# A fused attention and MLP kernel: the first batch's norms reordered, and two thirds of the second batch's norms moved into its own attention

## The chip, the cores and the metric

The kernel runs on one core of one Trainium2 chip. The metric is device time in microseconds, the median of several executions. One execution was also taken by the hardware profiler; all durations below come from that one. Batches are numbered from 1 here (the code's `b` from 0).

## The reference

Attention with normed queries and keys, then an MLP. Shapes: 8 batches, 12 heads, 448 positions, head size 64, so 3584 tokens of width 768, and 2048 inner features. All inputs and the output are float32.

```python
def rmsnorm(x, g):
    rms = np.sqrt(np.mean(x * x, axis=-1, keepdims=True) + 1e-06)
    return x / rms * g
q_n, k_n = (rmsnorm(q, g_q), rmsnorm(k, g_k))
scores = np.matmul(q_n, k_n.transpose(0, 1, 3, 2)) / np.sqrt(64)
attn = softmax(scores)
x = np.matmul(attn, v)           # heads side by side: (3584, 768)
h = x @ w_in
out = gelu_tanh(h) @ w_out
```

## The kernel before, in words

**Tiling.** A batch's 448 positions are 4 tiles of 112. Heads go in pairs (6 pairs), since two heads of 64 fill 128 partitions. Loads, squares and norms go in chunks of 4 heads (2 pairs), 3 chunks to a batch. `rawqk` holds 4 chunks of q and 4 of k in float32, used in turn.

**Norm.** For a piece of q or k: squares (`square`, L113, on ACT or POOL), their sums over the head (`total`, L122, DVE), the root as exp(-0.5 ln(.)) (`rsqrt`, L129, two ACT instructions, `lg` and `rinv`), and the product with the root, which also casts to bfloat16 (`normed`, L144, DVE or POOL). Gains g_q and g_k are folded into one column `gcol` that multiplies the transposed keys only.

**Transposes.** Scores need q and k with the head on partitions. Batch 1 transposes on PE (`trans`, L153): 8 matmuls into one PSUM tile, then a copy to `qT` and the gain product to `kT`. Later batches use DMA transposes issued by SP (`dma_trans`, L178), one for q and one for k of a chunk, and `gain` (L189) on DVE. kT is one buffer for all batches, and so is qT.

**Attention.** `scores` (L196) makes a 112 x 896 tile of scores for a pair and a key tile, two matmuls, and one exp on ACT (L206). There are 24 such tiles in a batch. Two PSUM tiles (`ps_s`) take turns, so a score matmul waits for the exp two before it. The exp subtracts a constant `shift` made of the largest gain product in place of the row's maximum. `pair_sums` (L219) then makes the sums over keys (`what` 0, matmul with ones; on DVE two 32x32 transposes and a reciprocal, L241 to L243) and the product with V (`what` 1, then L236). A slot is half of a pair: two score tiles, and in batch 1 one of the two `pair_sums`. There are 12 slots.

**MLP.** `mm1` makes 128 inner features of a batch (6 matmuls and a gelu into `g`); in batch 1 `mm1_pair` (L290) makes 256 at a time. `mm2` (L261) makes 128 tokens by 384 outputs from 16 matmuls. Two batches share the halves of `g`; the mm2 of the batch before is spread over the attention of the next by counts (`attention`, L314).

**Order.** The order is written by hand: each engine executes its own instructions as the program emits them, and waits on semaphores. `plan` (L382) hangs small steps on slot numbers. `first_attention` (L353) runs batch 1's attention with the lists `side` (ahead of the slot's scores), `mid` (between its two score tiles) and `late` (behind `pair_sums`); then follows mm1 of batch 1 with the list `m1` by inner step, then batch 2's attention with its own `side`. SP issues all loads of q and k, the DMA transposes and the outputs, in one queue. POOL issues V, w_in and w_out (cast to bfloat16 on the way), between its squares and norms. A SP or POOL instruction whose buffer isn't free holds all that stands behind it.

**What the steps touch, before.** The start, L440 to L476: the gain column, `gall` by five DVE transposes, `shift`, then the first pair's squares, sums, root, norm, transposes. Batch 1's other pairs: squares and norms on POOL, roots in `mid`, transposes in `late`, pair hp + 1 in slot 2 hp. w_in comes in four parts (L472, L487, L490, L491), w_out in two halves (L494, L497). Batch 2: squares on POOL in slots 8 to 11 (four of six in unused parts of `g`), one root for all three chunks in mm1 (L508, with an activation table load before and after, since gelu and exp don't share a table), 12 norms on DVE (L513), the six DMA transposes, and only then (L541) batch 3's loads.

Of the kernel before, what the change touches and what calls it, by code (L numbers as in the profile page):

```python
# [16 lines left out]
def kernel(  # L17
# [54 lines left out]
    gall = consts.tile([128, 2, 32], F32)  # L72
    shift = consts.tile([P, 1], F32)
    eps = consts.tile([P, 1], F32)
    win = wts.tile([128, HP, d_ff], BF16)
# [63 lines left out]
    def idle(n, w):  # L139

        for _ in range(n):
            nc.tensor.matmul(w, zeros[:, :128], zeros, start=True, stop=True)
# [207 lines left out]
            pair_sums(b, HP - 1, what)  # L350
        upto(quota)

    def first_attention(side, mid, late):  # L353


        warm = {}
        for i in range(HP * 2):
            for fn in side.get(i, ()):
                fn()
            scores(0, i // 2, 2 * (i % 2))  # L360
            for fn in mid.get(i, ()):
                fn()
            scores(0, i // 2, 2 * (i % 2) + 1)
            if i < 2:
                warm[i] = ps_o.tile([128, S], F32, tag=f"o{i}", name=f"o{i}")
                idle((6, 2)[i], warm[i])
            if i >= 2:
                pair_sums(0, i // 2 - 1, i % 2, waits=1)
            for fn in late.get(i, ()):
                fn()  # L370
            if i == 1:
                idle(4, warm[i])
        nc.scalar.preload_act_table_set(GELU_SET)
        square(1, 2, "k", nc.scalar)
        pair_sums(0, HP - 1, 0)
        mm1_pair(0, range(HP - 1))
        pair_sums(0, HP - 1, 1)
        mm1_pair(1, range(HP - 1))
        for i in range(2):
            mm1_pair(i, range(HP - 1, HP))  # L380

    def plan(*entries):  # L382
        steps = {}
# [12 lines left out]
        qh[i]()  # L396
        kh[i]()
    loads(0, 2)
    loads(1, 0)
    loads(1, 1)  # L400
    load_v(0, 0, CH)
    nc.vector.memset(eps, 1e-6)
    nc.vector.memset(ones, 1.0)

    def pair(hp):
        return hp // (CH // 2), hp % (CH // 2), slice(2 * (hp % (CH // 2)), 2 * (hp % (CH // 2)) + 2)
# [30 lines left out]
            moe_w_out[:, i * HD:(i + 1) * HD].rearrange("(f p) d -> p f d", p=128),  # L437
        )

    w = ps_m.tile([128, 512], F32, tag="mm", name="w")[:, :S]  # L440
# [5 lines left out]
    for r in range(4):  # L446
        at = (r ^ 1) * 32
        nc.vector.transpose(
            gall[r * 32:(r + 1) * 32, 1], gcol[at:at + 32].to_broadcast([32, 32])
        )  # L450

    nc.vector.tensor_reduce(
        shift, gall[:P].rearrange("p a d -> p (a d)"), axis=AX.X, op=ALU.max,
        apply_absolute_value=True,
    )
    nc.vector.tensor_scalar(shift, shift, -(D ** 0.5), 60.0, op0=ALU.mult, op1=ALU.add)
    nc.vector.tensor_scalar(shift, shift, 0.0, None, op0=ALU.min)
    squares0(0, nc.scalar)
    totals0(0)
    square(0, 0, "q", nc.scalar, slice(2, 4))  # L460
    rsqrt0(0)
    square(0, 0, "k", nc.scalar, slice(2, 4))
    total(0, 0, "q", slice(2, 4))
    normed0(0, nc.vector)
    total(0, 0, "k", slice(2, 4))
    trans(0, 0, ps_m)
    idle(4, ps_m.tile([128, 512], F32, tag="mm", name="w")[:, :S])
    rsqrt0(1)
    squares0(2, nc.gpsimd)
    square(0, 1, "q", nc.gpsimd, slice(2, 4))  # L470
    w_in_part(0, 4)
    normed0(1, nc.gpsimd)  # L472
    square(0, 1, "k", nc.gpsimd, slice(2, 4))
    load_v(0, CH, CH)
    squares0(4, nc.gpsimd)
    totals0(2)  # L476


    free = g[:P].rearrange("p f s -> p (f s)")
    for i, (n, c) in enumerate((n, c) for c in (1, 2) for n in "qk"):  # L480
        at = nf * 2 * S - (4 - i) * 2048
        sqs[n, 1, c] = free[:, at:at + 2048].bitcast(F32).rearrange(
            "p (h t d) -> p h t d", h=CH, t=NK
        )

    side = [(1, lambda: totals0(3)),
            (2, lambda: normed0(2, nc.gpsimd), lambda: w_in_part(1, 4),  # L487
             lambda: squares0(5, nc.gpsimd), lambda: totals0(4)),
            (4, lambda: normed0(3, nc.gpsimd), lambda: load_v(0, 2 * CH, CH),
             lambda: w_in_part(2, 4), lambda: totals0(5)),  # L490
            (6, lambda: normed0(4, nc.gpsimd), lambda: w_in_part(3, 4)),  # L491
            (7, lambda: loads(1, 2)),
            (8, lambda: normed0(5, nc.gpsimd), lambda: square(1, 0, "q", nc.gpsimd)),
            (9, lambda: square(1, 0, "k", nc.gpsimd), lambda: w_out_part(0)),  # L494
            (10, lambda: square(1, 1, "q", nc.gpsimd), lambda: total(1, 0, "q")),
            (11, lambda: square(1, 1, "k", nc.gpsimd), lambda: total(1, 0, "k"),
             lambda: load_v(1, 0, CH), lambda: w_out_part(1),  # L497
             lambda: square(1, 2, "q", nc.gpsimd))]
    mid = [(1, lambda: rsqrt0(2))] + [
        (2 * hp - 3, lambda hp=hp: rsqrt0(hp)) for hp in range(3, HP)]  # L500
    late = [(1, lambda: trans(0, 1, ps_m))] + [
        (2 * hp, lambda hp=hp: trans(0, hp + 1, ps_m)) for hp in range(1, HP - 1)]
    first_attention(plan(*side), plan(*mid), plan(*late))
    for c in (1, 2):
        for n in "qk":
            total(1, c, n)

    def rsqrt1():  # L508
        nc.scalar.preload_act_table_set(EXP_SET)
        rsqrt(1)  # L510
        nc.scalar.preload_act_table_set(GELU_SET)

    def normed1(c):  # L513
        for j in range(CH // 2):
            for n in "qk":
# [100 lines left out]
```

## Time and profile before

| | us |
|---|---|
| median of 3 runs | 459.52 (458.99 to 459.62) |
| the profiled execution, its time | 458.26 |
| its span (first to last instruction) | 456.5 |
| first exp starts | 13.99 |
| last exp of batch 1 ends | 44.09 |
| mm1 of batch 1 done on PE | 65.5 |
| first scores of batch 2 | 67.17 |
| batch 2's attention done, mm1 of batch 2 starts | 103.3 |
| PE busy | 435.2 (95% of the span) |
| ACT busy | 306.2 (67%) |
| DVE busy | 252.7 (55%) |
| POOL busy | 154.2 (34%) |
| granted PE clock, mean | 0.996 |

The busy times are means over stages that differ. The first 103 us hold all loads of weights, the first batch without any other work to fill PE, and the second batch's norms; the remaining 353 us repeat one pattern. The profile's 40 slices are 11.4 us each.

### The profile page before, as it was taken

Reading aid. Unit: us, or ns where it says so; the run is one execution under the profiler, and the core shown is the slowest. Engines: PE = TensorE matmul, PEld = TensorE weight load, DVE = VectorE, ACT = ScalarE, POOL = GpSimd, SP = SyncE. Lnnn points to the kernel's source line nnn. Section 1 sums busy time; section 2 is a strip of 40 time slices with the busy share of each in tenths; the row PEclk is TensorE's granted clock in tenths of the full one; section 3 lists DMA queues with packets and bytes.
Section 4 is the critical chain, followed back from the end, with each engine's and each line's share of the span. In section 5 each row is a group of like instructions: output and inputs, shape, how many; then the busy total and the mean of one; then the engine's idle time right before and its main releaser. Section 6 shows DMA issues by size and latency. Waiting matters only on the chain.

```text
span 456.5 us, 7031 instructions
## 1 busy us (share of the span) xinstructions
PE 435.2 (95%) x2766; PEld 212.7 (47%) x2766; DVE 252.7 (55%) x429; ACT 306.2 (67%) x406; POOL 154.2 (34%) x136
## 2 busy tenths in 40 slices
PE   5789979899999999999999999999999999999995
PEld 2233434345544554445544554455544554455563
DVE  5667663963397536874297536874288602862000
ACT  3679567665888577875888577875788447873410
POOL 4989405554400923046400923046400920000000
PEclk9899999999999999999999999999999999999999
DMA  8999999918951586317951586316751541111022
GB/s 225 231 233 166 203 200 233 209 34 150 251 93 36 136 183 131 80 36 180 219 93 36 127 191 117 95 36 166 154 93 36 107 51 34 36 37 34 1 69 69
DMA packets 84193, 54.92 MB, mean 120 GB/s; under 512 B 41152, under 2 KB 80576, under 8 KB 84160
## 3 DMA queue, kind: packets, MB, share of 16 engines
q1 hardware_dynamic: 65792, 42.68, 39.2%
q0 software_dynamic: 18208, 11.80, 18.4%
q8 instruction: 21, 0.34, 0.3%
q14 instruction: 12, 0.10, 0.1%
q10 hardware_dynamic: 160, 0.00, 0.0%
HBM read 45.61 MB, written 11.01 MB: 124 GB/s over the span
## 4 chain that ended last, share of the span: by engine, by line
PE 84%; DVE 4%; ACT 4%; DMA 3%; POOL 3%; issue 1%; SPq 1%; DVEq 0%; POOLq 0%; ACTq 0%
PE o L268 32%; PE h L250 28%; PE o L229 13%; PE sc L202 9%; ACT ex L206 3%; DMA rawq<-in_q_dram 2%; POOL sq L120 2%; PE hh L298 1%; DVE ss L125 1%; DVE nrmq L147 1%; DVE nrmk L147 1%; DMA kT<-nrmk 1%; POOL nrmq L147 0%; POOL nrmk L147 0%; PE tp L164 0%
## 5 line engine op out<-in xcount | busy, mean ns | idle before, releaser
L206 ACT ACTIVATE ex<-sc,shift 112x896 bf16<-112x896 f32 x192 | 182.9, 1003 | 32.6 <-PE sc L202 31.5
L268 PE MATMUL o<-wout,g 128*128 128x384 bf16 x896 | 160.7, 327 | 0.0
L250 PE MATMUL h<-xT,win 128*128 128x448 bf16 x672 | 128.3, 352 | 0.0
L268 PEld LDWEIGHTS <-g 128*128 128x128 bf16 x896 | 80.6, 98 | 71.0 <-issue 24.1
L254 ACT ACTIVATE g<-h 128x448 bf16<-128x448 f32 x112 | 60.9, 544 | 76.3 <-PE h L250 73.4
L250 PEld LDWEIGHTS <-win 128*128 128x128 bf16 x672 | 65.8, 98 | 61.0
L147 POOL TENSOR_TENSOR nrmq<-rawq,rinv 112x512 bf16<-112x512 f32 x41 | 44.0, 1091 | 133.1 <-issue 123.2
L125 DVE TENSOR_REDUCE ss<-sq 112x16 f32<-112x1024 f32 (+1 forms) x50 | 53.5, 1086 | 64.1 <-ACT sq L118 55.1
L278 DVE COPY osb<-o 128x384 f32<-128x384 f32 x52 | 28.7, 551 | 75.4 <-PE o L268 75.4
L202 PE MATMUL sc<-qT,kT 64*128 64x448 bf16 x384 | 56.4, 357 | 5.8 <-ACT ex L206 2.0
L217 DVE TENSOR_TENSOR es<-ex 112x896 bf16<-112x896 bf16 x72 | 47.1, 654 | 2.7 <-ACT ex L206 1.7
L241 DVE STREAM_TRANSPOSE st<-o 128x448 f32<-128x448 f32 x48 | 31.1, 649 | 30.1 <-PE o L229 30.1
L120 POOL TENSOR_TENSOR sq<-rawq 112x1024 f32<-112x1024 f32 (+1 forms) x13 | 21.7, 1671 | 74.6 <-DMA rawq<-in_q_dram 43.0
L229 PE MATMUL o<-ex,vb 112*64 112x448 bf16 x384 | 44.8, 353 | 1.4 <-DVE xT L236 1.4
L147 POOL TENSOR_TENSOR nrmk<-rawk,rinv 112x512 bf16<-112x512 f32 x41 | 44.0, 1090 | 0.0
L202 PEld LDWEIGHTS <-kT 64*128 64x128 bf16 x384 | 16.6, 93 | 45.0 <-issue 36.0
L236 DVE TENSOR_TENSOR xT<-o,rb 128x448 bf16<-128x448 f32 x48 | 30.0, 624 | 6.2 <-PE o L229 1.8
L243 DVE STREAM_TRANSPOSE rb<-rc 128x448 f32<-128x448 f32 x48 | 31.0, 645 | 1.6
L229 PEld LDWEIGHTS <-vb 112*64 112x64 bf16 x384 | 22.5, 109 | 14.4 <-issue 3.5
L120 POOL TENSOR_TENSOR sq<-rawk 112x1024 f32<-112x1024 f32 (+1 forms) x13 | 21.7, 1668 | 5.2 <-DVE ss L125 4.3
L229 PE MATMUL o<-es,ones 112*64 112x448 bf16 x144 | 21.6, 366 | 0.1
L229 PEld LDWEIGHTS <-ones 112*64 112x64 bf16 x240 | 11.8, 108 | 18.7 <-issue 16.2
(52 smaller groups left out, 205.1 us busy)
## 6 DMA issues: line engine op xcount, KB each, us to landing
rawq<-in_q_dram SPq DMA_DIRECT2D x22, 448.0 KB, 5.4
rawk<-in_k_dram SPq DMA_DIRECT2D x22, 448.0 KB, 5.8
vb<-in_v_dram POOLq DMA_DIRECT2D x6, 672.0 KB, 7.2
win<-in_moe_w_in_dram POOLq DMA_DIRECT2D x4, 768.0 KB, 9.4
wout<-in_moe_w_out_dram POOLq DMA_DIRECT2D x2, 1536.0 KB, 13.5
out_dram<-osb SPq DMA_DIRECT2D x8, 336.0 KB, 2.8
out_dram<-osb SPq DMA_DIRECT2D x8, 288.0 KB, 2.7
out_dram<-osb SPq DMA_DIRECT2D x8, 240.0 KB, 2.7
```

What stands on the lines that cost most here:

```text
L120: eng.tensor_mul(sq, raw, raw)
L125: nc.vector.reduce_sum(sss[b][:, c, "qk".index(n), hs], sqs[n, b, c][:, hs], axis=AX.X)
L147: eng.tensor_mul(nrms[n, b, c][:, j].rearrange("p t a d -> p a t d"), raws[n, b, c][:, 2 * j:2 * j + 2], rinvs[b][:, c, "qk".index(n), 2 * ...
L202: nc.tensor.matmul(sc[:, a, :S], kT[r, hp, kt], qT[b][r, hp], start=True, stop=True,)
L206: nc.scalar.activation(exs[b, hp][:, kt], sc[:P, :, :S], AF.Exp, scale=scale, bias=shift)
L217: nc.vector.tensor_add(ess[b, hp][:, i], ex[:, 2 * i], ex[:, 2 * i + 1])
L229: nc.tensor.matmul(o[a * D:(a + 1) * D], vb[b % 2][:, 2 * hp + a, i] if what else ones, e[:, i, a], start=(i == 0), stop=(i == n - 1),)
L241: nc.vector.transpose(st.rearrange("p a b -> p (a b)"), o)
L243: nc.vector.transpose(oas["rb"], rc.to_broadcast([128, S // 32, 32]))
L250: nc.tensor.matmul(h[:, :S], win[:, c, f * 128:(f + 1) * 128], xT[b][:, c], start=(c == 0), stop=(c == HP - 1),)
L254: nc.scalar.activation(g[:, f, (b % 2) * S:(b % 2 + 1) * S], h[:, :S], AF.Gelu_apprx_tanh)
L268: nc.tensor.matmul(o[:, :HD], g[:, f, i * 128:(i + 1) * 128], wout[:, f, half * HD:(half + 1) * HD], start=(f == 0), stop=(f == nf - 1),)
```

## The change

At the start, squares, sums and root of the first pair come ahead of the gain column; `shift` comes from one small matmul (ones by a diagonal of gains in bfloat16, hence a margin of 2^-8) in place of five DVE transposes. The other squares of batch 1's chunks 2 and 3 mostly go to unused parts of `g` and not to the two-buffer pool. The second pair's norm goes from POOL to DVE. Batch 1's transposes move from slot 2 hp - 2 to slot 2 hp - 1, ahead of the product with V (pair 3: behind it). The warming matmul in front of `pair_sums` stays only in slots 2 to 5. w_in's second part moves behind the fifth pair's norm, its third and fourth behind the last norm and two squares of batch 2. The pairs of mm1 are no longer cut around the last product with V.

Batch 2's chunk 1 gets a root of its own in slot 11 and is normed on DVE and transposed at the start of mm1. Chunks 2 and 3 get their root (no table loads of its own) and their norms, now on POOL, at the start of batch 2's attention, the transposes of chunk 2 behind that and those of chunk 3 in slot 4. The loads of batch 3's chunks 1 and 2 stand on SP right behind the first transposes, its chunk 3 behind the second, and batch 4's chunk 1 (slot 1) and the first output pieces also stand ahead of the third. The sums of batch 3's squares come some slots later. A dummy `rawqk` tile is taken, so that the chunks keep the buffers that they had.

```diff
-    def first_attention(side, mid, late):
+    def first_attention(side, mid, early, late):
...
-            if i >= 2:
-                pair_sums(0, i // 2 - 1, i % 2, waits=1)
-            for fn in late.get(i, ()):
+            for fn in early.get(i, ()):
                 fn()
             if i == 1:
                 idle(4, warm[i])
+            if i >= 2:
+                pair_sums(0, i // 2 - 1, i % 2, waits=i < 6)
+            for fn in late.get(i, ()):
+                fn()
         nc.scalar.preload_act_table_set(GELU_SET)
         square(1, 2, "k", nc.scalar)
-        pair_sums(0, HP - 1, 0)
-        mm1_pair(0, range(HP - 1))
-        pair_sums(0, HP - 1, 1)
-        mm1_pair(1, range(HP - 1))
+        for what in range(2):
+            pair_sums(0, HP - 1, what)
         for i in range(2):
-            mm1_pair(i, range(HP - 1, HP))
+            mm1_pair(i)
...
-    loads(1, 0)
-    loads(1, 1)
-    load_v(0, 0, CH)
+    for n in "qk":
+        rawqk.tile([P, CH, NK, D], F32, tag=f"raw{n}", name=f"raw{n}")
...
-    idle(20, w)
+    idle(16, ps_m.tile([128, 512], F32, tag="mm", name="w")[:, :S])
+    squares0(0, nc.scalar)
+    totals0(0)
+    rsqrt0(0)
     for a in range(2):
         nc.vector.tensor_mul(gcol[a * D:(a + 1) * D], grow[:, 0:1], grow[:, 1:2])
-    nc.vector.transpose(gall[:, 0], gcol.to_broadcast([128, 32]))
...
+    nc.vector.tensor_scalar(gdiag, ident[:D, :D], gcol[:D, 0:1], None, op0=ALU.mult)
+    gall = ps_o.tile([128, S], F32, tag="o1", name="gall")
+    nc.tensor.matmul(gall[:P, :D], rows, gdiag, start=True, stop=True)
...
+    side = [(1, lambda: normed0(1, nc.vector), lambda: total(0, 1, "k", slice(0, 2)),
+             lambda: loads(1, 0)),
+            (2, lambda: rsqrt0(2), lambda: normed0(2, nc.gpsimd),
+             lambda: load_v(0, CH, CH), lambda: square(0, 2, "k", nc.gpsimd, slice(0, 2)),
+             lambda: totals0(3)),
+            (4, lambda: normed0(3, nc.gpsimd), lambda: squares0(5, nc.gpsimd),
+             lambda: totals0(4), lambda: loads(1, 1)),
+            (6, lambda: normed0(4, nc.gpsimd), lambda: w_in_part(1, 4),
+             lambda: load_v(0, 2 * CH, CH), lambda: totals0(5)),
+            (8, lambda: normed0(5, nc.gpsimd), lambda: square(1, 0, "q", nc.gpsimd),
+             lambda: square(1, 0, "k", nc.gpsimd), lambda: w_in_part(2, 4),
+             lambda: w_in_part(3, 4), lambda: loads(1, 2)),
+            (10, lambda: square(1, 1, "q", nc.gpsimd), lambda: total(1, 0, "k")),
+            (11, lambda: square(1, 1, "k", nc.gpsimd), lambda: w_out_part(0),
+             lambda: load_v(1, 0, CH), lambda: square(1, 2, "q", nc.gpsimd),
+             lambda: w_out_part(1))]
+    mid = [(0, lambda: rsqrt0(1))] + [(2 * hp - 3, lambda hp=hp: rsqrt0(hp)) for hp in range(3, HP)]
+    early = [(2 * hp + 1, lambda hp=hp: trans(0, hp + 1, ps_m)) for hp in (0, 2, 3, 4)]
+    mid.append((11, lambda: rsqrt(1, 0)))
+    late = [(3, lambda: trans(0, 2, ps_m)), (9, lambda: total(1, 0, "q"))]
...
         if b == 0:
-            m1 = [(2, rsqrt1)]
-            for c in range(NCH):
-                m1 += [(2 + c, lambda c=c: normed1(c)), (3 + c, lambda c=c: transposed(1, c))]
-            m1 += [(5, lambda: load_v(1, CH, CH)),
-                   (6, lambda: gain(1, 0), lambda: load_v(1, 2 * CH, CH)),
-                   (7, lambda: loads(2, 0), lambda: loads(2, 1), lambda: loads(2, 2))]
-            side += [(0, lambda: gain(1, 1)), (3, lambda: gain(1, 2))]
+            m1 = [(1, lambda: normed1(0), lambda: transposed(1, 0), lambda: loads(2, 0),
+                   lambda: loads(2, 1), lambda: total(1, 1, "q"), lambda: total(1, 1, "k")),
+                  (3, lambda: load_v(1, CH, CH), lambda: load_v(1, 2 * CH, CH)),
+                  (4, lambda: total(1, 2, "q"), lambda: total(1, 2, "k")),
+                  (6, lambda: gain(1, 0))]
+            side += [(0, lambda: rsqrt(1, slice(1, NCH)), lambda: normed_all(1, 1),
+                      lambda: normed_all(1, 2), lambda: transposed(1, 1), lambda: loads(2, 2)),
+                     (3, lambda: gain(1, 1)), (4, lambda: transposed(1, 2)),
+                     (7, lambda: gain(1, 2))]
             for c in range(NCH):
                 side += [
-                    (2 * c, lambda c=c: square(2, c, "q", nc.gpsimd)),
-                    (2 * c, lambda c=c: square(2, c, "k", nc.gpsimd)),
-                    (2 * c + 2, lambda c=c: total(2, c, "q")),
-                    (2 * c + 3, lambda c=c: total(2, c, "k")),
+                    (2 * c + 1, lambda c=c: square(2, c, "q", nc.gpsimd)),
+                    (2 * c + 1, lambda c=c: square(2, c, "k", nc.gpsimd)),
+                    (2 * c + 5, lambda c=c: total(2, c, "q")),
+                    (2 * c + 6, lambda c=c: total(2, c, "k")),
                 ]
```

More of the change, by code (lines that the diff above doesn't have):

```diff
@@ L71 @@
     gcol = consts.tile([128, 1], F32)
-    gall = consts.tile([128, 2, 32], F32)
+    gdiag = consts.tile([D, D], BF16)
+    rows = consts.tile([D, P], BF16)
     shift = consts.tile([P, 1], F32)
@@ L398 @@
     loads(0, 2)
-    loads(1, 0)
-    loads(1, 1)
-    load_v(0, 0, CH)
+    for n in "qk":
+        rawqk.tile([P, CH, NK, D], F32, tag=f"raw{n}", name=f"raw{n}")
     nc.vector.memset(eps, 1e-6)
     nc.vector.memset(ones, 1.0)
+    nc.vector.memset(rows, 1.0)
+    free = g[:P].rearrange("p f s -> p (f s)")
+    for i, (n, b, c) in enumerate((("q", 0, 1), ("k", 0, 1), ("q", 0, 2),
+                                   ("q", 1, 1), ("k", 1, 1), ("q", 1, 2), ("k", 1, 2))):
+        sqs[n, b, c] = free[:, i * 2048:(i + 1) * 2048].bitcast(F32).rearrange(
+            "p (h t d) -> p h t d", h=CH, t=NK
+        )
     def pair(hp):
@@ L438, in w_out_part @@
         )
-    w = ps_m.tile([128, 512], F32, tag="mm", name="w")[:, :S]
-    idle(20, w)
+    idle(16, ps_m.tile([128, 512], F32, tag="mm", name="w")[:, :S])
+    squares0(0, nc.scalar)
+    totals0(0)
+    rsqrt0(0)
     for a in range(2):
         nc.vector.tensor_mul(gcol[a * D:(a + 1) * D], grow[:, 0:1], grow[:, 1:2])
-    nc.vector.transpose(gall[:, 0], gcol.to_broadcast([128, 32]))
[L446 to L450, printed above, removed]
+    nc.vector.tensor_scalar(gdiag, ident[:D, :D], gcol[:D, 0:1], None, op0=ALU.mult)
@@ L452 @@
+    gall = ps_o.tile([128, S], F32, tag="o1", name="gall")
+    nc.tensor.matmul(gall[:P, :D], rows, gdiag, start=True, stop=True)
+    idle(3, ps_m.tile([128, 512], F32, tag="mm", name="w")[:, :S])
+    square(0, 0, "q", nc.scalar, slice(2, 4))
+    normed0(0, nc.vector)
     nc.vector.tensor_reduce(
-        shift, gall[:P].rearrange("p a d -> p (a d)"), axis=AX.X, op=ALU.max,
-        apply_absolute_value=True,
-    )
-    nc.vector.tensor_scalar(shift, shift, -(D ** 0.5), 60.0, op0=ALU.mult, op1=ALU.add)
+        shift, gall[:P, :D], axis=AX.X, op=ALU.max, apply_absolute_value=True
+    )
@@ L457 @@
+    nc.vector.tensor_scalar(
+        shift, shift, -(D ** 0.5) * (1 + 2.0 ** -8), 60.0, op0=ALU.mult, op1=ALU.add
+    )
     nc.vector.tensor_scalar(shift, shift, 0.0, None, op0=ALU.min)
[L458 to L461, printed above, removed]
+    trans(0, 0, ps_m)
+    idle(3, ps_m.tile([128, 512], F32, tag="mm", name="w")[:, :S])
     square(0, 0, "k", nc.scalar, slice(2, 4))
-    total(0, 0, "q", slice(2, 4))
-    normed0(0, nc.vector)
-    total(0, 0, "k", slice(2, 4))
@@ L466 @@
[L466 to L470, printed above, removed]
-    w_in_part(0, 4)
[L472 to L511, printed above, removed]
+    totals0(1)
@@ new lines @@
+    square(0, 1, "q", nc.gpsimd, slice(0, 2))
+    load_v(0, 0, CH)
+    square(0, 1, "k", nc.gpsimd, slice(0, 2))
+    w_in_part(0, 4)
+    squares0(3, nc.gpsimd)
+    square(0, 2, "q", nc.gpsimd, slice(0, 2))
+    total(0, 1, "q", slice(0, 2))
+    side = [(1, lambda: normed0(1, nc.vector), lambda: total(0, 1, "k", slice(0, 2)),
[14 more added lines that the diff above has]
+             lambda: w_out_part(1))]
@@ L513, in normed1 @@
+    mid = [(0, lambda: rsqrt0(1))] + [(2 * hp - 3, lambda hp=hp: rsqrt0(hp)) for hp in range(3, HP)]
+    early = [(2 * hp + 1, lambda hp=hp: trans(0, hp + 1, ps_m)) for hp in (0, 2, 3, 4)]
+    mid.append((11, lambda: rsqrt(1, 0)))
+    late = [(3, lambda: trans(0, 2, ps_m)), (9, lambda: total(1, 0, "q"))]
+    first_attention(plan(*side), plan(*mid), plan(*early), plan(*late))
     def normed1(c):
```

## The prediction

> **What bounds it now.** I read the page's slices first, then busy time by stage, then the chain in time, then single transfers. Batches are numbered from 1; a chunk is 4 heads (1, 2, 3); a slot is half of a head pair's attention (0 to 11). The slices:
>
> ```profile
> PE   5789979899999999999999999999999999999995
> ...
> DMA  8999999918951586317951586316751541111022
> GB/s 225 231 233 166 203 200 233 209 34 150 251 93 36 136 183 131 80 36 180 219 93 36 127 191 117 95 36 166 154 93 36 107 51 34 36 37 34 1 69 69
> ```
>
> From slice 9 on (103 us) PE is at 90% or more and DMA has room: steady state. In the first eight slices DMA is full as well, at 200 to 230 GB/s. By stage (columns: stretch, length, busy time of PE, PEld, DVE, ACT and POOL with counts, PE clock, DMA share, GB/s):
>
> ```profile
> 20.00:44.10 24.10, 20.19 (x168) 8.18 (x165) 16.87 (x33) 19.92 (x26) 21.42 (x21) 1.00 1.12 207
> 44.10:67.10 23.00, 20.04 (x110) 9.73 (x106) 15.35 (x23) 13.35 (x15) 6.88 (x6) 1.00 1.33 198
> 67.10:103.10 36.00, 33.13 (x239) 15.93 (x240) 23.27 (x37) 25.20 (x28) 19.02 (x14) 1.00 0.74 160
> ...
> 121.50:456.50 335.00, 330.06 (x2097) 164.27 (x2096) 179.75 (x304) 226.07 (x299) 86.11 (x74) 1.00 0.43 94
> ```
>
> The last row holds 98.5% PE, and the change touches nothing there: any gain must come before 103.1. The first mm1 stage (44.1 to 67.1) ends in a wait for transfers. From the chain:
>
> ```profile
> 64.93 3.28 DMA kT<-nrmk
> 68.21 0.02 issue
> 68.23 0.46 DVE kT L192
> 68.69 0.17 SPq L187
> 68.86 0.05 issue
> 68.91 0.02 SPq L93
> 68.93 0.03 issue
> 68.96 5.06 DMA rawq<-in_q_dram
> ```
>
> So I read transfers one by one (tile, queue, count, KB, us to landing): wout's second half, issued at 46.49; two thirds of batch 2's V, issued at 49.53 and 50.3; the first qT, issued at 58.29; batch 4's first k, issued at 74.95; batch 3's V, issued at 77.84:
>
> ```profile
> wout<-in_moe_w_out_dram POOLq DMA_DIRECT2D x1, 1536.0 KB, 15.1
> ...
> vb<-in_v_dram POOLq DMA_DIRECT2D x2, 224.0 KB, 14.0
> ...
> qT<-nrmq SPq DMA_TRANSPOSE x1, 7.0
> ...
> rawk<-in_k_dram SPq DMA_DIRECT2D x1, 448.0 KB, 11.6
> ...
> vb<-in_v_dram POOLq DMA_DIRECT2D x1, 672.0 KB, 12.2
> ```
>
> They land at 61.6, about 64.8, 65.3, 86.5 and 90.0: in the order of issue, across SP's and POOL's queues. The qT took 7.0 where a later kT (issued at 64.93) took 3.3; it stood behind V. The first load after the transposes lands at 74.0, the eighth at 86.5. So the first 90 us are one line of transfers, almost without a gap (42 to 44: 43 GB/s while wout had just been issued at 40.81). What is late in that line is late for PE.
>
> **The change, part by part.**
>
> *Start.* Before, DVE makes gain and shift (5.76 to 7.82) ahead of the first sums; lg runs at 9.04, the first exp at 13.99. After: squares end at 4.07 and 4.89, two sums (0.62 to 0.69) 5.6, lg 0.31 and rinv 0.21: 6.2. Norms 0.69 + 0.60: 7.6. Last transposes 0.4: 8.0. qT copy 0.53, kT 0.45 with gaps: 9.1. Scores: exp at 9.7, that is 4.3 earlier. nrmk took 1.53 at 10.23 because POOL's square ran (9.69 to 11.22); now the norms end before that square can start (its load lands at 7.9). The new shift: gdiag and a 112x64 matmul have no row; gain's 0.15 and the small transposes' 0.21 bound the first, a score matmul's 0.36 and zero the second; I take 0.2 and 0.1. With the max 0.22 and two of 0.15 it ends at 8.2, hidden behind the transposes; uncovered it costs at most 0.6. `rows` memset and fewer idle matmuls: nothing, PE waits there.
>
> *First attention.* Before, exps run from 13.99 to 44.09; a pair takes 4.78 (28.80, 33.58, 38.35), of which 4 x 0.955 + 0.43 for the root is 4.25 and the rest a wait for scores behind the transposes and kT. After, transposes stand before the V product, one slot ahead of their scores: trans 0.6, copy 0.38, kT 0.45 fit beside the second exp and the root. The floor is 24 x 0.955 + 6 x 0.43 = 25.5. DVE's sums still hold the second pair (about 1.5), POOL's norms the third (1.2), and I leave 0.2 per pair: last exp ends near 38.8. Squares in g drop a buffer wait; they cost the same 1.04.
>
> *First mm1.* Now V product, sums and pairs in plain order: PE waits about 1.2 for DVE (st 0.65, rc 0.24, rb 0.65, xT 0.62). The root of batch 2's chunk 1 moves into slot 11 (0.65), chunks 2 and 3 into the next attention: two table loads (1.28 each) and one root go, ACT is off the path there. 96 matmuls at 0.188 = 18.0, and 0.9 for the V product: mm1 ends near 58.6, against 65.5. Eight DVE norms (0.60 each) become POOL's (1.03 each, 8.2): they run after the root at 61.5, done near 70. POOL loses nothing else by it.
>
> So the engines would be 7 us ahead. **The line of transfers is not.** Bytes are the same; order and gaps change.
>
> *Gap.* win's parts 3 and 4 moved behind the last norms and batch 2's squares on POOL. The last root comes near 29.0 (slot 7), norms 2.06: 31.1, two squares 3.8: issue at 34.9 (before: 28.75 and 32.34). By then all before it has landed, as before at 35.0 (V's third part: issue 27.99, 7.1). wout flowed some 2.6 after its issue; the same here gives 37.5, so the line stands still for about 2.9, and 1.0 more if the pairs slip by the 0.25 that half of today's wait is. I take 3.9 (bounds 1.5 and 6). The gap of before (1.6) goes, since wout is now issued at about 40 to 41, before win has landed.
>
> *Order.* SP now issues, after batch 2's first transposes: batch 3's chunks 1 and 2, transposes 2, batch 3's chunk 3, batch 4's chunk 1, the first two output pieces, and only then transposes 3, which slot 8 needs. POOL issues batch 3's V ahead of them too. Before, all six transposes stood ahead of these loads and had landed by 71.6. Work from 35.0 on until transposes 3 have landed:
> - win parts 3, 4: 7.7 (35.0 to 42.7);
> - wout twice 7.7 (53.9 to 61.6), V 1.2 + 1.6 + 1.6: 19.8;
> - six transposes at 0.9 (four from 64.8 to 68.2): 5.4;
> - eight loads at 1.79 (74.0 to 86.5 is seven): 14.3;
> - batch 3's V with the outputs: 3.5 (86.5 to 90.0).
> Sum 50.7. 35.0 + 3.9 + 50.7 = 89.6; gain 0.45 and a start 0.1: slot 8 at 90.2. Before, it started at 88.96. From there to the end of the stage before took 14.3 (PE 14.0 of it): I leave that, as the last slots are PE's.
>
> *Is PE there by then?* First transposes land between 65 (right behind wout) and 68.2 (behind V): start 65.6 to 68.8 against 67.17. Slots 0 to 3 took 10.1, and PE has by then idled 7 us. After 3.2 us idle (7.2 to 10.4) PE's clock was 0.58 and 0.57 in 12 to 16, so about 2 more: slot 4 at 77.7 to 80.9 (transposes 2 land at 77.2). Slots 4 to 7 took 11.7, 3.0 of it waits on DVE's sums and xT that the later sums mostly remove: 8.9. Slot 8 could start at 86.6 to 89.8. The transfer comes last, by little.
> The Trainium skill (TensorE: Matmul & The Clock Gate, Part 1) puts the way back to full clock at about 3.4 us of steady work; by that the price is 1.7 where I have 2, and the sum stays.
>
> *Sum*: 90.2 - 88.96 = **+1.2 us**. On the profiled execution (span 456.5, time 458.26) that is 459.5; its time lies 1.26 below the median of the runs, 459.52, so on the median I forecast **460.7**.
>
> **The rivals.**
> - *Transfers do not bind (faster).* If transposes land soon after issue, attention 2 starts when ACT has its root (61.5; scores at 59) and takes the 33 to 35 that PE has to do: end at 94 to 97 instead of 103.3, 6 to 9 less: about **453**. For it: engines are 7 us ahead; against: landings in order of issue. If only batch 3's V stays behind transposes 3, 3.5 goes from the sum, slot 8 starts when PE is there (87 to 88): 458.
> - *Queues share (slower).* If SP's loads are served beside POOL's line and not behind it, the first transposes land near 52, but four loads (7.2), chunk 2's transposes and chunk 3's loads halve wout's pace from 47 on: the second half lands near 76 instead of 63. Its first use is matmul 17 of slot 0; PE stands there until 76, slots 1 to 7 take 16, slot 8 starts near 92.7: +3.7, **463.2**. It decides once wout lands after 71. Against: V of batch 3 lands after, not among, the loads.
> The Trainium skill (DMA: Bandwidth & Descriptors, Queues, rings and completion order) says that each DMA engine takes turns between queues by packet. That is this rival; the landings above speak for order of issue.
> - *The first attention gains less than it says.* POOL and DVE norms block each other (1.53 for 0.69), and each us by which win's third part is issued later is a us on slot 8: at 38 instead of 34.9 the result is 463 to 464.
>
> **Numbers.** Forecast, order of issue binds (-1 to +2.5): 0.45, a third of it within the bound. Faster rivals 0.12 for free transfers, 0.15 for V passed. Slower: shared queues 0.13, a late POOL 0.15. About 0.2% (0.9 us) is what a measurement of this kernel tells from no change. Faster 0.28, same 0.20, slower 0.52. The range leaves out most of the free-transfer case: 456.3 to 464.2.
>
> **What would show it.** First exp near 9.7, last near 38.8, mm1's matmuls done near 58.6; win's third part issued near 35 with a slice of low GB/s before it; transposes 3 landing after batch 3's V, near 90; PE idle ahead of slot 8, released by kT's gain. Wrong if slot 8 starts well before 87, or if wout's second half is what PE waits for.

## The result, and the profile after

The changed kernel takes 462.91 us in the median of four runs (462.01 to 463.80), the kernel before 459.25 beside it: a ratio of 1.0081, 95% interval [1.0058, 1.0104], so 3.7 us slower. (All ratios below are to the kernel before, run beside each kernel.) The profiled execution took 463.38 us, its span is 461.6. mm1 of batch 2 starts at 108.42 (before: 103.29), and from there to the end both kernels take 353.2: the whole difference arises ahead of it (5.1 us in these two executions, 3.7 in the medians).

The slices of the page after (11.5 us each):

```profile
PE   7688943999999999999999999999999999999995
...
PEclk9899985999999999999999999999999999999999
DMA  8999999905991394606971394505861431111022
GB/s 215 249 184 151 193 243 188 257 1 117 228 177 35 72 223 62 168 0 136 253 133 34 78 238 54 156 14 142 192 95 36 94 61 35 36 34 36 1 68 68
```

The sixth and seventh digit of PE's row (58 to 81 us), 7 and 9 before, are 4 and 3 now, with the granted clock at 5 in the second of them, while DMA is full. By stage (rest of the first attention, mm1, batch 2's attention, the rest; columns as in the prediction):

```profile
15.60:39.73 24.13, 20.94 (x168) 8.51 (x167) 19.35 (x39) 20.78 (x30) 20.97 (x20) 0.94 0.99 184
39.73:59.95 20.22, 19.75 (x106) 9.83 (x105) 11.69 (x14) 8.76 (x9) 8.92 (x8) 1.00 1.27 195
59.95:108.42 48.47, 34.79 (x241) 16.16 (x241) 22.48 (x37) 27.39 (x31) 26.50 (x22) 0.86 0.87 162
126.60:461.60 335.00, 330.08 (x2097) 164.27 (x2096) 180.03 (x304) 226.07 (x299) 87.57 (x75) 1.00 0.44 94
```

The first exp comes 4 us earlier (9.96), the first mm1 ends 5.5 earlier (59.95), and batch 2's attention starts at 60.0 instead of 67.17. Then this one stage takes 48.5 us instead of 36: it loses 12.3, more than the 7.2 won. What it lost them to is in PE's timeline (start, us, engine, line, operation, tiles, count, idle time before and its releaser):

```profile
61.26 2.77 PE L269 MATMUL o<-wout,g 128*128 128x384 bf16 x16
76.31 1.44 PE L269 MATMUL o<-wout,g 128*128 128x384 bf16 x4 [12.28 <-DMA wout<-in_moe_w_out_dram]
77.68 0.93 PE L203 MATMUL sc<-qT,kT 64*128 64x448 bf16 x4
78.54 2.35 PE L269 MATMUL o<-wout,g 128*128 128x384 bf16 x10
```

and in the chain in order of time:

```profile
46.03 30.24 DMA wout<-in_moe_w_out_dram
76.27 0.04 issue
76.31 1.44 PE o L269 x4
```

The first 16 matmuls use wout's first half; the 17th stands 12.28 us for the second, which took 30.2 us from issue to landing where it took 15.1 before, and comes at 76.3 instead of 61.6. The four matmuls behind the wait take 1.44 where they take 0.7 at full clock. No slot makes the loss good, and slot 8 starts at 94.18. In the kernel before, the same 20 matmuls of wout ran without a wait:

```profile
67.65 3.42 PE L268 MATMUL o<-wout,g 128*128 128x384 bf16 x20
```

The single transfers (issue time in front of each, from the trace: first qT 44.39, first kT 46.66, batch 3's fourth load 54.76, the qT of chunk 2 65.01, batch 3's V 70.93):

```profile
qT<-nrmq SPq DMA_TRANSPOSE x1, 10.2
...
kT<-nrmk SPq DMA_TRANSPOSE x1, 12.8
...
rawk<-in_k_dram SPq DMA_DIRECT2D x1, 448.0 KB, 18.0
...
qT<-nrmq SPq DMA_TRANSPOSE x1, 12.4
...
vb<-in_v_dram POOLq DMA_DIRECT2D x1, 672.0 KB, 16.8
```

SP's first qT was issued behind wout's first half (41.75), its first kT and batch 3's loads behind the second (46.03). They landed at 54.6, 59.5 and 62 to 73, the halves of wout at 59.7 and 76.3. That isn't the order of issue. Summing the trace's packets of data by queue gives the rates in GB/s and the counts of packets:

| stretch | POOL's queue | SP's queue |
|---|---|---|
| before, 54 to 60 | wout (768 B packets): 205, 1600 packets | nothing |
| after, 52 to 56 | wout (768 B): 145, 755 | transposes (256 B): 46, 721 |
| after, 60 to 64 | wout (768 B): 105, 545 | batch 3's loads (1024 B): 143, 560 |
| before, 23.5 to 24.5 | V (512 B): 91, 178 | batch 2's loads (1024 B): 161, 157 |

Both queues flow at once, with nearly as many packets from the one as from the other, so the ratio of their rates is near that of their packets' sizes (46/145 = 0.32 for 256/768 = 0.33; 105/143 = 0.73 for 0.75): they take turns packet by packet. The Trainium skill (DMA: Bandwidth & Descriptors, Queues, rings and completion order) says that each DMA engine goes round between queue rows by packet; the counts in the trace agree. The last row is of the kernel before.

### The profile page after: what moved, and what is told of

Same layout as the page of the kernel before. It is cut to its first block, busy times and chain, and to the rows that moved or that the text cites. A ratio compares the mean times of both kernels' runs of the same rounds, so it can differ in the third digit from the quotient of the medians.

```text
span 461.6 us, 7015 instructions
## 1 busy us (share of the span) xinstructions
PE 434.1 (94%) x2759; PEld 212.7 (46%) x2759; DVE 250.5 (54%) x420; ACT 304.2 (66%) x406; POOL 161.5 (35%) x142
## 4 chain that ended last, share of the span: by engine, by line
PE 80%; DMA 8%; DVE 5%; POOL 4%; ACT 2%; issue 1%; ACTq 0%; DVEq 0%; POOLq 0%
PE o L269 31%; PE h L251 28%; PE o L230 11%; PE sc L203 9%; DMA wout<-in_moe_w_out_dram 7%; DVE ss L126 1%; POOL g L121 1%; ACT ex L207 1%; DMA grow<-in_g_k_dram 1%; POOL sq L121 1%; DVE nrmk L148 1%; DVE xT L237 1%; DVE rb L244 1%; POOL win L440 1%; DVE st L242 1%
## 5 line engine op out<-in xcount | busy, mean ns | idle before, releaser
L269 PE MATMUL o<-wout,g 128*128 128x384 bf16 x896 | 162.2, 329 | 12.4 <-DMA wout<-in_moe_w_out_dram 12.3
L269 PEld LDWEIGHTS <-g 128*128 128x128 bf16 x896 | 80.9, 98 | 84.0 <-issue 37.5
L148 POOL TENSOR_TENSOR nrmq<-rawq,rinv 112x512 bf16<-112x512 f32 x44 | 47.1, 1088 | 142.2 <-issue 121.8
L126 DVE TENSOR_REDUCE ss<-sq 112x16 f32<-112x1024 f32 (+1 forms) x44 | 49.5, 1142 | 58.3 <-ACT sq L119 58.2
L203 PE MATMUL sc<-qT,kT 64*128 64x448 bf16 x384 | 57.4, 359 | 5.4 <-ACT ex L207 2.4
L242 DVE STREAM_TRANSPOSE st<-o 128x448 f32<-128x448 f32 x48 | 31.1, 648 | 46.6 <-PE o L230 46.6
L148 POOL TENSOR_TENSOR nrmk<-rawk,rinv 112x512 bf16<-112x512 f32 x44 | 47.1, 1089 | 0.0
L121 POOL TENSOR_TENSOR sq<-rawq 112x1024 f32<-112x1024 f32 x9 | 18.1, 2007 | 62.2 <-DVE ss L126 42.5
L203 PEld LDWEIGHTS <-kT 64*128 64x128 bf16 x384 | 17.3, 94 | 46.8 <-issue 38.8
L121 POOL TENSOR_TENSOR sq<-rawk 112x1024 f32<-112x1024 f32 (+1 forms) x11 | 19.5, 1769 | 1.3 <-POOL sq L121 0.8
```

The lines of the kernel that those rows point to most:

```text
L121: eng.tensor_mul(sq, raw, raw)
L126: nc.vector.reduce_sum(sss[b][:, c, "qk".index(n), hs], sqs[n, b, c][:, hs], axis=AX.X)
L148: eng.tensor_mul(nrms[n, b, c][:, j].rearrange("p t a d -> p a t d"), raws[n, b, c][:, 2 * j:2 * j + 2], rinvs[b][:, c, "qk".index(n), 2 * ...
L203: nc.tensor.matmul(sc[:, a, :S], kT[r, hp, kt], qT[b][r, hp], start=True, stop=True,)
L242: nc.vector.transpose(st.rearrange("p a b -> p (a b)"), o)
L269: nc.tensor.matmul(o[:, :HD], g[:, f, i * 128:(i + 1) * 128], wout[:, f, half * HD:(half + 1) * HD], start=(f == 0), stop=(f == nf - 1),)
```

## The experiments

### One kind of SP's transfers out of wout's way: e1_loads_behind

```diff
-            m1 = [(1, lambda: normed1(0), lambda: transposed(1, 0), lambda: loads(2, 0),
-                   lambda: loads(2, 1), lambda: total(1, 1, "q"), lambda: total(1, 1, "k")),
+            m1 = [(1, lambda: normed1(0), lambda: transposed(1, 0),
+                   lambda: total(1, 1, "q"), lambda: total(1, 1, "k")),
...
-                      lambda: normed_all(1, 2), lambda: transposed(1, 1), lambda: loads(2, 2)),
+                      lambda: normed_all(1, 2), lambda: transposed(1, 1), lambda: loads(2, 0),
+                      lambda: loads(2, 1), lambda: loads(2, 2)),
```

> The changed kernel, with batch 3's loads of chunks 1 and 2 moved on SP from the start of the first mm1 to behind the transposes of batch 2's chunk 2. POOL's order and the first transposes stay. Theory 'queues share' (wout's second half was late, 76.3 instead of 61.6, since it took turns with SP's loads from 50 to 71): it lands at 62 to 65, PE's 12.3 us in front of the wout matmuls shrink below 3, chunk 2's transposes (issued near 65 to 67) land by 73 instead of 81; chunk 3's transposes still stand behind ten issues of SP and land near 88 to 90, so slot 8 starts at 88 to 90 and the time is 457 to 459.5. Rival 'POOL's own work slows its queue' (squares and norms on POOL, not the loads): wout still lands near 76, time 462 to 463. Rival 'the first two transposes slow it' : wout near 70 to 76, time 460 to 463. Rival 'order of issue' as forecast: wout near 62 and slot 8 at 90.2, but then the changed kernel itself should have shown wout near 62, and it did not.

Measured: 461.31 us, ratio [1.0031, 1.0079]. POOL's order is untouched, yet wout's second half lands 7.9 us earlier, at 68.4, and PE waits 3.98 for it instead of 12.28. So the loads did hold wout up, and POOL's own work, whose rows are the same in both up to 71 us, did not; but it is 3 to 6 later than I expected (a gap in the line, see e6, and the first two transposes, which also share with wout: 46 GB/s of 191 from 52 to 56 in the changed kernel). Chunk 3's transposes, behind the loads on SP, land at 90.8, PE waits 4.2 for them, and slot 8 starts at 91.3.

### All loads behind all transposes: e2_loads_last

e1, with `transposed(1, 2)` moved from slot 4 to directly behind `transposed(1, 1)`.

> The changed kernel with all of batch 3's loads on SP behind all six transposes: the transposes of batch 2's chunk 3 move from slot 4 to right behind those of chunk 2, the loads of chunks 1 to 3 behind both. 'Queues share': wout's second half at 62 to 65, transposes 2 by 73, transposes 3 by 78, nothing that batch 2's attention needs stands behind a load; slot 8 then starts when PE is there, at 83 to 86, mm1 of batch 2 near 97 to 100 instead of 108.6, time 451 to 456. 'Order of issue' (transfers in one line): transposes 3 land near 75, the same slot 8, time 452 to 456; it differs from sharing in wout alone. 'POOL's own work slows its queue': wout at 76 as in the changed kernel, time 460 to 462. If batch 3's loads come too late instead (its squares and norms are due in batch 2's attention), POOL's squares wait and the loss shows up in batch 3, not in batch 2.

Measured: 461.02, ratio [1.0014, 1.0068]; 5 us more than expected, though transposes 3 now land at 77.4. DVE's timeline shows why slot 8 still starts at 88.3:

```profile
81.87 1.22 DVE L126 TENSOR_REDUCE ss<-sq 112x16 f32<-112x1024 f32 x1 [2.77 <-POOL sq L121]
83.90 1.22 DVE L126 TENSOR_REDUCE ss<-sq 112x16 f32<-112x1024 f32 x1 [0.81 <-POOL sq L121]
...
86.73 0.62 DVE L237 TENSOR_TENSOR xT<-o,rb 128x448 bf16<-128x448 f32 x1
87.27 1.02 DVE L193 TENSOR_SCALAR kT<-kT,gcol 128x896 bf16<-128x896 bf16 x1
```

The gain (L193) had its data ten microseconds earlier. It stood in DVE's order behind two sums of batch 3's squares, and POOL made those squares late because batch 3's loads were now late:

```profile
79.94 1.90 POOL L121 TENSOR_TENSOR sq<-rawq 112x1024 f32<-112x1024 f32 x1 [9.57 <-DMA rawq<-in_q_dram]
```

A wait for a transfer had become a wait in another engine's queue.

### The gain ahead of those sums: e5_gain_early

e2 with `gain(1, 2)` in slot 5 instead of 7.

> As e2_loads_last, but the gain on the keys of batch 2's chunk 3 stands in slot 5 of DVE's order instead of slot 7, ahead of the sums of batch 3's squares. In e2_loads_last its transposes landed at 77.4 and slot 8 still began at 88.3. Theory 'DVE's order': the gain stood behind two sums that waited for POOL's squares and these for batch 3's late loads (80.7 to 87.3 in DVE's rows). Then slot 8 starts when PE is there, 83.5 to 85, mm1 of batch 2 at 99.5 to 102 instead of 105.0, profiled time 454.5 to 457. Rival 'the transfer': the gain is released late by its DMA wherever it stands, slot 8 stays near 88, time 460 to 461.

Measured: 457.33, ratio [0.9956, 0.9992], slot 8 at 84.4: 3.7 us from the position of one DVE instruction. mm1 of batch 2 starts at 102.1, at the late end of what I expected: the sums still stood ahead of the work of slot 8 on DVE (4.8 us from slot 8 to slot 9, where before had 2.4).

### The two halves of the change alone: e3_front_only, e4_back_only

e3 is the changed start and first attention with the old back half (one root with table loads, 12 norms on DVE, six transposes, then loads). e4 is the reverse.

> Start and first attention of the changed kernel; norms, transposes and loads of batches 2 and 3 as before (one root for three chunks in mm1 with its two table loads, 12 norms on DVE, six transposes, then the loads). 'Queues share': transposes are issued near 54 to 60 and share with wout and V only, land at 59 to 68; wout at 64 to 67; batch 2's attention starts near 62 to 64 and nothing holds it later; time 452 to 455. 'Order of issue': the six land behind wout and V at 66 to 73, attention starts near 67, time 457 to 459. If the front part brings nothing by itself (its gain is eaten by the later weights), 459.

> Start and first attention as before; only batch 2's norms split (own root for chunk 1 in slot 11, chunks 2 and 3 rooted and normed on POOL in batch 2's attention) with SP's order of transposes and loads as in the changed kernel. 'Queues share': wout's second half near 72 to 76 instead of 61.6, PE waits for it in slot 0, chunk 2's transposes land near 82 to 86, chunk 3's near 92 to 95; mm1 of batch 2 near 108 to 111; time 463 to 467, slower than the changed kernel, which has the better front. 'Order of issue': wout at 61.6 as before, chunk 3's transposes near 88 to 90, time 459 to 461.

Measured: e3 461.27, ratio [1.0033, 1.0081]; e4 463.18, ratio [1.0058, 1.0119]. Neither half gains alone. e3 came out slower than either theory had it: its first transposes were issued at 53.1 and 54.6, 5 us earlier than before, but shared with wout, and the kT took 13.3 us. PE's timeline:

```profile
68.38 0.93 PE L203 MATMUL sc<-qT,kT 64*128 64x448 bf16 x4 [7.98 <-DVE kT L193]
69.24 5.93 PE L269 MATMUL o<-wout,g 128*128 128x384 bf16 x20
```

Attention 2 starts later than before (68.4 against 67.2), and after 8 idle us its first 20 matmuls take 5.93 where the same 20 take 3.42 in e7. Ending mm1 early only bought a colder clock (granted 0.50 from 68 to 74). e4's time came as expected, though not in the expected way: its wout was in time (its loads are issued at 58 to 62, when wout is nearly through), and it lost its time at slot 8 (91.8), where the last kT stood behind the loads and batch 3's V.

### The gap: e6_win_early, e8_front_win_early

In `side`, w_in's parts each go one step earlier on POOL: part 2 behind `normed0(3)` in slot 4, part 3 behind V in slot 6, part 4 ahead of batch 2's squares in slot 8. e6 is the changed kernel with this edit alone, e8 is e3 with it.

```diff
-            (4, lambda: normed0(3, nc.gpsimd), lambda: squares0(5, nc.gpsimd),
+            (4, lambda: normed0(3, nc.gpsimd), lambda: w_in_part(1, 4), lambda: squares0(5, nc.gpsimd),
...
-            (6, lambda: normed0(4, nc.gpsimd), lambda: w_in_part(1, 4),
-             lambda: load_v(0, 2 * CH, CH), lambda: totals0(5)),
-            (8, lambda: normed0(5, nc.gpsimd), lambda: square(1, 0, "q", nc.gpsimd),
-             lambda: square(1, 0, "k", nc.gpsimd), lambda: w_in_part(2, 4),
-             lambda: w_in_part(3, 4), lambda: loads(1, 2)),
+            (6, lambda: normed0(4, nc.gpsimd), lambda: load_v(0, 2 * CH, CH),
+             lambda: w_in_part(2, 4), lambda: totals0(5)),
+            (8, lambda: normed0(5, nc.gpsimd), lambda: w_in_part(3, 4),
+             lambda: square(1, 0, "q", nc.gpsimd), lambda: square(1, 0, "k", nc.gpsimd),
+             lambda: loads(1, 2)),
```

> The changed kernel with w_in's parts 2, 3 and 4 each one step earlier in POOL's order (behind the fourth, fifth and sixth pair's norm; part 4 ahead of batch 2's squares), nothing else. Theory 'the gap' : the transfers stood almost still at 28 to 31 and at 36 to 39 because POOL issued these parts late, some 4 us in all; with them issued near 24, 30 and 33 wout's second half lands at 72 to 74 instead of 76.3, slot 1 starts near 75, and all behind it comes 2 to 4 earlier: 459 to 461. Rival 'sharing sets wout's end alone': wout's second half lands within 1 of 76.3 and the time stays at 462 to 463.5. If the issues hold up POOL's norms, the last exp of batch 1 comes up to 2 later than 39.7.

> e3_front_only (changed start and first attention, back half as before) with w_in's parts one step earlier. In e3_front_only PE stood 7.98 us ahead of batch 2's first scores until the first kT had landed and been gained (68.3). Theory 'the line of transfers is what the front half waits for': the first kT lands 3 to 5 earlier, slot 0 at 63.5 to 65.5, mm1 of batch 2 at 101 to 103 instead of 105.7, time 456 to 459. Rival 'the cold clock': PE's slow restart is what costs; with a shorter wait it restarts as slowly, and no more than 1.5 is won: 459.5 to 461.

Measured: e6 456.85, ratio [0.9943, 0.9986], so 6.1 us less than the changed kernel and faster than the kernel before; more than I expected. In the changed kernel POOL issued w_in's second part at 28.39 (before: 23.09) and its last parts at 36.3 and 37.2:

```profile
34.50 1.88 POOL L121 TENSOR_TENSOR sq<-rawk 112x1024 f32<-112x1024 f32 x1
36.33 1.72 POOL L440 DMA_DIRECT2D win<-in_moe_w_in_dram  x2
```

and the packets fell to 13, 24 and 153 GB/s from 28.8 to 31.8 (us by us) and to 90, 0, 34 and 174 from 35.8 to 39.8. Against 200 GB/s that is an estimated 4.6 us of empty line. In e6 it is closed (206 GB/s and more in all these stretches) and wout's second half lands at 68.9, 7.4 earlier: the gap itself, and in addition more of wout passes before batch 3's loads come to share (2.47 of its 3.15 MB by their first packet, 1.57 in the changed kernel). e8 has the expected time (458.61, ratio [0.9969, 1.0008], 2.7 less than e3), but its profiled execution can't say by what: there the first attention ended 2.3 later than in e3 and batch 2's first scores started at 69.2, no earlier (68.4 in e3). PE had waited 1.60 for V's first third until 19.96, and from 22.3 to 28.7 its matmuls took up to twice their time (1.71 for eight that take 0.95; granted clock 0.52).

### Both together, and what was then late: e7_gain_and_win, e9_sums_late

e7 is e5 with w_in's parts early.

> Both edits on e2_loads_last: the gain of chunk 3 in slot 5 and w_in's parts one step earlier. If the three causes (queues that share, the gap, DVE's order) are separate, the gains add: wout's second half at 62 to 64, PE's 4.0 us wait for it and the cold clock behind it mostly gone, slot 8 at 79.5 to 83, mm1 of batch 2 at 96 to 99, time 451 to 455, faster than before by 1 to 1.7%. If instead the last of them hides the others, it ends where e5_gain_early does, 454.5 to 457.

Measured: 458.92, ratio [0.9982, 1.0032]: a miss, and a telling one. wout lands at 63.6 (12.7 us earlier than in the changed kernel; the two edits bring 7.9 and 7.4 alone), PE doesn't wait for it, and slot 8 starts at 79.65, 9.3 us earlier than before. Then PE stops:

```profile
79.65 0.67 PE L203 MATMUL sc<-qT,kT 64*128 64x448 bf16 x4
86.63 1.70 PE L230 MATMUL o<-ex,ones 112*64 112x448 bf16 x8 [6.31 <-DVE st L242]
88.32 1.71 PE L230 MATMUL o<-ex,vb 112*64 112x448 bf16 x8
```

DVE, the engine named, was itself idle 4.34 us until 82.96, waiting for POOL's square of batch 3, in the same two sums as in e2. The `st` of the pair before (L242) stands behind them. e9 moves them:

```diff
+        for fn in side.get(2 * HP, ()):
+            fn()
...
-                    (2 * c + 5, lambda c=c: total(2, c, "q")),
-                    (2 * c + 6, lambda c=c: total(2, c, "k")),
+                    ((9, 11, 12)[c], lambda c=c: total(2, c, "q"), lambda c=c: total(2, c, "k")),
...
-            side += [(11, lambda: rsqrt(b + 2)),
+            side += [(11 if b else 12, lambda: rsqrt(b + 2)),
```

(slot 12 is a new place behind the last slot, ahead of the table load.)

> As e7_gain_and_win, with one thing more moved on DVE: the sums of batch 3's squares, which stood in slots 5 to 10 of batch 2's attention, come in slots 9 and 11 and behind the last slot, and batch 3's root behind them, before the table for gelu is loaded. In e7_gain_and_win slot 8 began at 79.6, 9.4 earlier than before, and then PE stood 6.31 (to 86.63) for the sums over keys, which on DVE stood behind two sums that waited for POOL's squares and these for batch 3's loads. Theory 'DVE's order': the wait and the half clock behind it go; slot 9 starts near 81.5, the last slot near 88, mm1 of batch 2 at 94 to 97 instead of 103.1, profiled time 449 to 452. Rival 'batch 3's data are late for whoever comes next': the wait moves into the root, so mm1 of batch 2 or batch 3's attention starts late by what was won, time 456 to 459.

Measured: **452.73 us, ratio 0.9874 [0.9847, 0.9902]**, faster than both kernels; the profiled execution took 452.59, just above the 449 to 452 expected, and mm1 of batch 2 starts at 96.44. The stages of e9 (mm1, batch 2's attention, the rest):

```profile
39.84:62.00 22.16, 19.75 (x106) 9.81 (x105) 11.77 (x14) 10.47 (x11) 7.27 (x7) 1.00 1.23 171
62.00:96.44 34.44, 32.84 (x240) 15.92 (x241) 21.34 (x35) 24.65 (x30) 20.36 (x16) 1.00 1.03 203
96.44:450.80 354.36, 348.59 (x2194) 173.31 (x2191) 188.20 (x315) 239.28 (x323) 102.66 (x87) 1.00 0.47 99
```

Attention 2 takes 34.4 with PE busy for 32.8 of it at full clock. The rest is 1.2 longer than elsewhere (353.2), and all of that lies in mm1 of batch 2 (19.4 from its start to batch 3's first scores, 18.3 before): PE waits there 0.74 for DVE's `xT`, which now stands behind the late sums. That is much less than the rival's price.

### The direct question: e10_one_load_early

The kernel before, with `loads(2, 0)` at the start of the first mm1 instead of behind the transposes.

> The kernel before, with one edit: batch 3's loads of chunk 1 (q and k, 0.92 MB) are issued on SP at the start of the first mm1 (near 46 to 48) instead of behind the six transposes. It asks only how SP's loads stand to wout, which POOL has issued or is issuing by then. 'Queues share': the loads land by 58, while wout's second half is on its way, and that half lands 3 to 4.5 later than the 61.6 of before; transposes and slot 0 move by about as much, time 460 to 462. 'Order of issue': the loads land behind wout (after 62), wout stays at 61.6. In both the transposes come later than before, so the time tells less than the landings.

Measured: 462.93, ratio [1.0069, 1.0114]. The edit did something else than I wrote: SP was free and issued the loads at 35.9 and 36.9, beside w_in and ahead of wout, so wout's landing (62.4) tells nothing. But the queues can be seen sharing: from 40 to 42 w_in has 122 GB/s and the loads 125, at 1024 B packets on both sides. And since POOL's squares of batch 3 now had their data, POOL issued batch 3's V at 54.4 instead of 77.8. From 62 to 68 V (512 B) has 123 GB/s and the transposes (256 B) 59; the first kT comes 5 us later, attention 2 starts at 72.1. One load issued early in SP's queue let a transfer of POOL's queue loose on SP's transposes.

### What the changed front half is worth: e12_old_front

e9's back half behind the old start and first attention.

> Start and first attention as before, and the back half of e9_sums_late (own root for batch 2's chunk 1, norms on POOL in batch 2's attention, all transposes ahead of batch 3's loads, gain in slot 5, sums and root of batch 3 late). It asks what the changed first half is worth once nothing behind it holds its gain back. Theory: now the engines' order sets the end, so the 5 us that the changed front has at the end of the first mm1 (59.5 against 65.5) count in full: slot 0 at 67 to 68, mm1 of batch 2 near 101 to 103, time 456.5 to 459. Rival 'the transfers still set it': wout and the transposes come no earlier with the new front than with the old one, so this kernel ends where e9_sums_late does, 452 to 454.

Measured: 458.92, ratio 1.0002 [0.9985, 1.0019]: the time of the kernel before. With e9's back half the changed front, w_in's parts early, is worth 6.2 us (458.92 to 452.73). With the old back half the same front gains nothing that can be told from noise (e8), and with w_in late it costs 2 (e3). Its gain was real, and was lost behind it.

## Why the prediction was near in time and wrong in cause

The time on record, 460.7, is 2.2 below the one measured and on the right side of no change. But the change it forecast, +1.2, is a third of the 3.7 measured, and what it named as the cause is not what PE lost its time to. The rival "queues share" is: wout at 76 (76.3), slots 1 to 7 in 16 (16.5), slot 8 at 92.7 (94.18), 463.2 (462.91). It had a chance of 0.13. That the two times are near is partly luck: the two causes put slot 8 only 2.5 us apart, and the range, 456.3 to 464.2, holds both, so the time alone could not tell them apart. The limit that was forecast did stand one step behind: in the changed kernel transposes 3 landed at 92.7, behind batch 3's V (87.7), and in e1, where PE waits less for wout, PE stands 4.2 for them and slot 8 starts at 91.3 (forecast: 90.2).

- **Start, first attention, mm1.** 9.7, 38.8 and 58.6 were forecast; 9.96, 39.73 and 59.95 came. The new shift was hidden, as said. The second pair's norm on DVE took more than its row: 2.71 instead of 0.69, beside POOL's squares. The text had about 1.5 for what holds the second pair, and put it down to DVE's sums.
- **Gap.** Forecast: w_in's third part at 34.9, 3.9 us of standstill. Measured: 36.33, and 4.6 us in two pieces, 2.1 near 30 and 2.5 near 37. The first, from w_in's second part, stands nowhere in the working; that both together lie within the bounds of 1.5 and 6 is luck too. The text also missed that a gap moves wout into the loads, so that it counts 7.4 (e6) and not 4.6.
- **Order.** This step failed: "They land ... in the order of issue, across SP's and POOL's queues", and so "one line of transfers", in which wout's second half lands in time (63 in the working) and transposes 3 come last. It landed at 76.3, since SP's transfers took turns with it. In the rows read for this step, SP's first transposes had been issued 8 us and more behind the last of POOL's transfers, so the same landings follow from sharing. Nor did the first qT stand behind V: from 62.5 to 64.5 the trace has 960 packets of transposes beside 108 of V's, and V landed at 64.7 (V was at its end; why these counts are not equal is open). What made the qT look as if it stood in line is a start-up: its first packet came 4.0 us after its issue (58.29 to 62.33), just when wout had landed (61.6). In the changed kernel the first qT was issued at 44.39, in the middle of wout, and its first packet came 4.0 later all the same; in e7, with POOL's queue nearly empty, the third transpose needed 1.2 (64.73 to 65.91). The kernel before also had a stretch with work in both queues (23.5 to 24.5 us, last row of the table by queue), and it spoke for sharing.
- **Is PE there by then?** This assumed wout in time. With PE waiting 12.3 for it, slot 4 came at 85.05 instead of 77.7 to 80.9. The 2 us for the clock were about right: 1.44 + 0.93 + 2.35 for what takes 0.7 + 0.55 + 1.80 is 1.7.
- **From slot 8 on.** 14.3 was forecast, 14.24 measured.
- **Against the rival** the text held that V of batch 3 lands after the loads. V was issued 3 us behind the last of those loads, on a queue that had been idle, and its first packet came at 83.7. From 84 to 85 the trace has 169 of its packets beside 159 of the loads': it did run among them, and landed last because it began last. These rows speak for the rival, not against it.

The prediction's last line, wrong "if wout's second half is what PE waits for", is what happened. Settled are the sharing (rates, e1, e10), the gap (e6) and DVE's order (e5, e9). That the gains don't add in e7, whose median is above e6's and e5's, goes with its wait for DVE's sums (6.31 us of PE, 1.13 in e5), and e9, which moves these sums, is 6.2 below e7. Not settled is what e8's edit won, since its profiled execution was held up at its start by V.

## What to carry to other kernels

In these runs two DMA queues with work at once shared by packet, so small packets (DMA transposes) got the least, and a load "behind" a weight in time wasn't behind it if it stood on another queue. Before reading an order out of landings, look for a stretch in which both queues had work, and sum packets by queue there. When a stage ends early by moving work out of it, list what every in-order queue still holds for the next stage (transfers, but also sums and gains that stand behind another batch's late data); here three such things were late one behind the other, and each hid the next.

## What was not expected of the hardware

- Packet sizes set the shares: 46 GB/s against 145 for 256 and 768 B and 105 against 143 for 768 and 1024 B (the changed kernel), 59 against 123 for 256 and 512 B and 122 against 125 for equal ones (e10).
- The first transpose on SP's queue sent its first packet 3.9 to 4.1 us after its issue in every kernel traced here, while POOL's queue moved about 200 GB/s; a later one that found SP's queue empty needed 3.7 in e1 and e2 with POOL's queue as full, and 1.2 in e7, where it moved 81 GB/s. In e9 it moved 177 in that time and the figure is 1.2 too, so what sets it stays open.
- A DVE product of two operands took 2.71 us instead of 0.69 while three POOL squares ran back to back, from 12.56 to 16.05 (the last took 1.49 instead of 1.04). The changed kernel's row is the first below; the sum behind it, of one operand, took its usual 0.67 beside the last of these squares.

```profile
12.45 2.71 DVE L148 TENSOR_TENSOR nrmk<-rawk,rinv 112x512 bf16<-112x512 f32 x1
15.09 0.67 DVE L126 TENSOR_REDUCE ss<-g 112x8 f32<-112x512 f32 x1
```
